# Transposes of late tokens issued when they are ready, one norm per group moved to GpSimd, mask loads moved to SyncE, convolution turns taken one chunk sooner

## Chip, cores, metric

One core of a Trainium2 chip. The metric is the device time of one launch in microseconds (us); the profile's span leaves out some 1.8 us of it. Engines: PE (TensorE), ScalarE (ACT in the profile), VectorE (DVE), GpSimd (POOL) and SyncE (SP, which here only issues DMA). The kernel before took 560.66 us (median of 4 runs, 559.19 to 561.94).

## The reference, cut

Four residual layers on a 2048 x 512 bf16 sequence: long convolution (S4), local attention, and both once more with the same weights.

```python
x = A_u
x = x + _A_ref(_layernorm(x), A_re, A_im, B_re, B_im, C_re, C_im, log_dt, Dskip)   # FFT convolution of length 2L
x = x + _B_ref(_layernorm(x), B_wqkv, B_wo)
x = x + _A_ref(...)        # the same again
x = x + _B_ref(...)

def _B_ref(x, wqkv, wo):   # 32 heads of 16; each token sees 8 tokens at distance 0, 2, .., 14
    qkv = (x @ wqkv) ...
    logits = einsum(q, k[idx]) * 16 ** -0.5; masked where idx < 0
    return (softmax(logits) @ v[idx]) @ wo
```

## The kernel before, the parts that matter

The tokens lie in four groups of four slots (512 tokens each). In an attention layer `KS` and `QS` hold the rows of K and Q as the logits read them, `st` the rows on their way there, and `xnT` holds the normalized, transposed tokens (its name in the profile is XU). Groups 0 and 1 (the even half) are made in a prologue, groups 2 and 3 (the odd half) while the loop runs, by `late`. The loop has 36 steps, nine for each of four row sets `n`; sets `n` = 0 and 1 need only groups 0 and 1, sets 2 and 3 need groups 2 and 3.

```python
class LnStats:
    def gather(self, X, part, j0, j1):              # bn_stats on VectorE, one per slot
    def aggregate(self, j0, j1, half=None):         # bn_aggr on VectorE; with half: power 0.5 (a square root, "the power" below) in two GpSimd instructions
    def scales(self, j0, j1):                       # reciprocal and bias on VectorE, after the power
    def norm(self, dst, src, j, eng=None):          # VectorE, or GpSimd if given

# a projection: rows of K or Q for set n; the copies into KS/QS go by SyncE's queue
def proj(n, k, eng=on_dve):
    par, fp = n // 2, n % 2
    ...
    ps = gps([128, 512])
    for ct in range(4):
        nc.tensor.matmul(ps[:], wqk[...], xnT[:, ct, par, ...], ...)
    eng(st[n, which][...], ps[:])
    if h or n == 0:
        for e in range(2):
            nc.sync.dma_start(T[e::2, e, f2, ...], st[n, which][e::2, ...])

# PE, VectorE and ScalarE run in the order written; the order of GpSimd and SyncE is the scheduler's
with tc.manual_schedule(engines={PE, DVE, Activation}):
    def late(t):                                    # called at the end of step t
        for g in (2, 3):
            u, m0 = t - 2 * g + 4, g * 4            # group 2: steps 0..3, group 3: steps 2..5
            if u in (0, 1):   gather two slots, all parts
            elif u == 2:      ln_b.aggregate(m0, m0 + 4, C["half"])
            elif u == 3:
                ln_b.scales(m0, m0 + 4)
                four norms on GpSimd into xq[g]
                two nc.sync.dma_start_transpose(xt[...], xq[g][...])
                four nc.gpsimd.tensor_copy(xnT[...], xt[...])
    ... prologue: norms, transposes on PE, first rows of set 0 ...
    for t in range(36):
        end = min(total, max(need, done + (4 if t < 4 or t >= N - 8 else 3)))   # projection units of this step
        logits(t)            # PE reads KS, QS; exponential on ScalarE
        square()
        work(end - 1, t)
        values(t - 2)        # PE; reciprocal and product on VectorE
        ...
        turn_o(t // 3 - 1)   # every third step: transpose by SyncE, copy by GpSimd
        late(t)
```

The second convolution is a software pipeline over 16 chunks: `s1(k)` first transform (PE, evacuated into a Z tile), `turns(k)` two chunks' transposes by SyncE, `s2`, `product` (VectorE), `inverse`, `final`. Masks (the fixed rows of KS and QS) and two weights were issued from GpSimd's queue (`eng = nc.gpsimd`).

The softmax here doesn't subtract the row's maximum and nothing guards it: scores larger than these inputs give would overflow.

Of the kernel before, what the change touches and what calls it, by code (L numbers as in the profile page):

```python
# [14 lines left out]
BF = mybir.dt.bfloat16  # L15
# [146 lines left out]
def load_b_weights(nc, const, wq_in, C, wqkv, wo):  # L162
# [6 lines left out]
    wsrc = wqkv.rearrange("(t p) f -> p t f", p=128)  # L169
    eng = nc.gpsimd  # L170
    mask = nc.inline_tensor(_bf(_mask_rows()), name="c_mask").ap()
# [522 lines left out]
def kernel_and_first_conv(nc, tc, C, prm, x2d, const, kt_dram, kscr, ln, ln_b, W, wq_src):  # L694
    with ExitStack() as es:
# [100 lines left out]
        with tc.manual_schedule(engines={mybir.EngineType.PE}):  # L796
# [11 lines left out]
            for u in range(2):  # L808
                cv.block(2 + u, xc, Kt, VT, 10 if u == 0 else 4)
            ln_b.gather(X, 0, 0, 8)  # L810
            nc.scalar.activation(cv.one.tile([128, 1], F32, name="pre", tag="pre")[:], C["half"][:, 0:1], ACT.Sqrt)
# [5 lines left out]
def a_layer(nc, tc, C, X, kt_dram, XU, ln_b, finish):  # L817

    with ExitStack() as es:
# [45 lines left out]
        def turns(k):  # L865
            turn(nc, zpair(k), Z[k // 4], (k % 4) * 4, 8)
# [72 lines left out]
        with tc.manual_schedule(engines={mybir.EngineType.PE, mybir.EngineType.DVE, mybir.EngineType.Activation}):  # L939
            s1(0, on_dve)  # L940
            finish()
            s1(1, on_act)
            s1(2, on_dve)
            s1(3, on_act)
            zpair(0)
            warm(2)
            turn_pe(0)
            s1(4)
            s2(0, True)
            turns(2)  # L950
            turn_pe(1)
            for i in range(16):
                if 0 < i < 7:
                    s2(i)
                if 6 <= i < 15:
                    s2(i + 1)
                product(i)
                if i == 15:
                    inverse(14, True)
                    inverse(15)  # L960
                if 0 < i < 15:
                    inverse(i - 1, i > 10)
                if i == 0:
                    s1(5, on_dve)
                if i + 6 < 16:
                    s1(i + 6)
                    if i % 4 == 1:
                        turns(i + 3)
                        turns(i + 5)
                if i >= 5:  # L970
                    final(i - 5, on_dve if i in (6, 8) else on_act)
                if 10 <= i < 14:
                    ln_b.gather(X, 0, 2 * i - 20, 2 * i - 18)
                if i >= 14:
                    ln_b.gather(X, 1, 4 * i - 56, 4 * i - 52)
            for k in range(11, 16):
                final(k)


def b_layer(nc, tc, C, X, Wt, ln_b, XU, store=None, ln_next=None):  # L980

    with ExitStack() as es:
# [40 lines left out]

        def normed(g, acts):
            xn = []
            for i in range(4):
# [5 lines left out]
                else:  # L1032
                    ln_b.norm(xn[i][:], X[:, slot(j), :], j)
            return xn
# [175 lines left out]
        with tc.manual_schedule(engines={mybir.EngineType.PE, mybir.EngineType.DVE, mybir.EngineType.Activation}):  # L1210
# [8 lines left out]
            def late(t):  # L1219
                for g in (2, 3):  # L1220
                    u, m0 = t - 2 * g + 4, g * 4
                    if u in (0, 1):
                        for p in range(len(ln_b.parts)):
                            ln_b.gather(X, p, m0 + 2 * u, m0 + 2 * u + 2)
                    elif u == 2:
                        ln_b.aggregate(m0, m0 + 4, C["half"])
                    elif u == 3:
                        ln_b.scales(m0, m0 + 4)
                        xq[g] = ld.tile([128, 4, D], BF, name="xq", tag="xq")
                        for i in range(4):  # L1230
                            ln_b.norm(xq[g][:, i], X[:, slot(m0 + i), :], m0 + i, nc.gpsimd)
                        xt = ld.tile([128, 16, 128], BF, name="xt", tag="xt")
                        for h in range(2):
                            nc.sync.dma_start_transpose(xt[:, 8 * h:8 * h + 8],
                                                        xq[g][:, 2 * h:2 * h + 2].rearrange("p i d -> p (i d)"))
                        for ct in range(4):
                            dst = xnT[:, ct, g // 2, UF:UF + 1024].rearrange("c (p j) -> c p j", j=8)
# [10 lines left out]
            warm(6)  # L1248
            ln_b.gather(X, last, 4, 8)
            ln_b.scales(0, 4)  # L1250
            xn = normed(0, (3,))
            ln_b.aggregate(4, 8)
            root(1)
            pt0 = turned(xn)
            ln_b.scales(4, 8)
            fan(0, pt0, 0)
            xn = normed(1, (3,))
            warm(4)
            pt1 = turned(xn)
            pre = sm.tile([128, 1], F32, name="pre", tag="pre")  # L1260
            nc.scalar.activation(pre[:], C["half"][:, 0:1], ACT.Exp)
# [10 lines left out]
            odd = begun(3, psO)  # L1272
            placed(0, half[0], FIRST, 512)
            spread(3, odd, on_dve)
            placed(2, half[1], FIRST, 512)
            jobs = []
            for n in range(4):
# [4 lines left out]
                jobs += [(NB * n + b // 2 + 1 + b / 100, 1, vproj(p, n % 2, b), 0 if n < 2 else 13) for b in range(NB)]  # L1282
            jobs += [(N - 9 + .8 * m, 2, out(m), 24) for m in range(8)]
            jobs.sort(key=lambda j: j[0])
# [23 lines left out]
            for t in range(N):  # L1308
                need = max([c for d, c in due if int(d) <= t] + [0])
                end = min(total, max(need, done + (4 if t < 4 or t >= N - 8 else 3)))  # L1310
                if t:
# [138 lines left out]
```

## Time and profile before

| stage of the kernel before | us of the span |
|---|---|
| tables and first convolution, to the first prologue statistic | 256.5 |
| prologue of attention layer 1 | 11.1 |
| layer 1: steps 0-8, step 9, 10-27, 28-34 (exponential to exponential) | 31.05, 3.43, 40.90, 18.38 |
| end of layer 1, to the first product of the second convolution | 23.4 |
| second convolution: product 0 to product 15, then to layer 2's first exponential | 48.4, 16.5 |
| layer 2: the same four stretches, and the tail | 31.90, 3.60, 40.49, 18.07, 15.6 |

An undisturbed step takes 2.23 us, so the nine steps 0 to 8 hold over 10 us too much. The page's group for all 72 exponentials shows it from ScalarE's side: busy time and mean of one, then the idle time ahead of them (up to 0.54 us in an even step is part of it) and who ended it.

```profile
L1121 ACT ACTIVATE PT<-S 128x1824 bf16<-128x1824 f32 x72 | 121.8, 1691 | 52.4 <-PE S L1118 52.2
```

### The profile page before, as it was taken

How to read it: one execution, taken by the hardware profiler on the slowest of the kernel's cores; microseconds unless marked ns; L12 is line 12 of the kernel's file. 1: busy time of each engine (PE TensorE's matmuls, PEld its weight loads, DVE VectorE, ACT ScalarE, POOL GpSimd, SP SyncE). 2: the span in 40 equal slices, each digit the busy share in tenths (PEclk: the TensorE clock that was granted, in tenths of full speed). 3: DMA queues.
4: the chain of work that ended last, by engine and by line, in shares of the span. 5: the costliest groups of instructions: out<-in, count | busy, mean ns of one | idle time of the engine just before them, and what ended most of it. 6: DMA issues, size and time to landing. Idle time of an engine off the chain costs nothing.

```text
span 559.4 us, 15229 instructions
## 1 busy us (share of the span) xinstructions
PE 394.0 (70%) x6465; PEld 259.0 (46%) x6526; DVE 429.3 (77%) x967; ACT 354.5 (63%) x435; POOL 85.2 (15%) x137
## 2 busy tenths in 40 slices
PE   0200665585668459698976999777897797699977
PEld 0100433464337136465544566545565554366654
DVE  4999999979989998776863666576978787266753
ACT  4999554355536247356654778966877766378771
POOL 0000000000000020533084101250000207411110
PEclk9999997789779688799997999887989999699999
DMA  8201057532463557344134334125863013434542
GB/s 275 110 1 37 2 113 98 85 124 54 99 115 114 115 80 223 53 150 153 67 81 114 87 69 87 15 85 115 170 132 66 2 57 73 110 77 86 115 68 77
DMA packets 99896, 52.51 MB, mean 94 GB/s; under 512 B 85235, under 2 KB 92788, under 8 KB 98548
## 3 DMA queue, kind: packets, MB, share of 16 engines
q1 hardware_dynamic: 97316, 47.73, 37.1%
q0 software_dynamic: 928, 3.41, 1.9%
q8 instruction: 51, 0.84, 0.6%
q10 hardware_dynamic: 1584, 0.39, 0.3%
q14 instruction: 17, 0.14, 0.1%
HBM read 17.96 MB, written 8.13 MB: 47 GB/s over the span
## 4 chain that ended last, share of the span: by engine, by line
PE 36%; DVE 22%; ACT 10%; DMA 5%; issue 3%; POOL 3%; SPq 2%; ACTq 0%; DVEq 0%; POOLq 0%
PE psG L1083 6%; ACT PT L1121 6%; DMA zt<-Z 5%; PE psG L1101 4%; PE S L1118 4%; PE O L1137 4%; PE psG L1172 3%; DVE Ytab L656 3%; DVE Y2tab L658 3%; DVE ln_st_b L212 2%; DVE ta L619 2%; DVE tb L620 2%; POOL XU L1238 1%; SPq L266 1%; POOL xq L260 1%
## 5 line engine op out<-in xcount | busy, mean ns | idle before, releaser
L1121 ACT ACTIVATE PT<-S 128x1824 bf16<-128x1824 f32 x72 | 121.8, 1691 | 52.4 <-PE S L1118 52.2
L1087 DVE CAST st<-psG 128x512 bf16<-128x512 f32 x56 | 38.3, 684 | 37.1 <-PE psG L1083 37.1
L1083 PE MATMUL psG<-XU,wqk 128*128 128x512 bf16 x196 | 57.8, 395 | 3.7 <-issue 1.6
L1118 PE MATMUL S<-QS,KS 32*128 32x114 bf16 x1152 | 28.8, 214 | 24.9 <-DMA KS<-st 15.7
L1137 PEld LDWEIGHTS <-PT 128*128 128x128 bf16 x1152 | 39.4, 97 | 13.9 <-DVE on L1145 2.5
L1118 PEld LDWEIGHTS <-KS 32*128 32x128 bf16 x1152 | 20.4, 94 | 49.5 <-issue 38.0
L1137 PE MATMUL O<-V,PT 128*128 128x17 bf16 x1152 | 40.4, 171 | 0.8 <-DVE on L1145 0.3
L1101 PE MATMUL psG<-wv,XU 128*128 128x256 bf16 x288 | 39.6, 273 | 0.6 <-ACT V L1103 0.6
L307 PE MATMUL psA<-X,sb_F 128*128 128x128 bf16 x128 | 13.5, 238 | 36.4 <-ACT X L720 35.2
L307 PEld LDWEIGHTS <-sb_F 128*128 128x128 bf16 x256 | 17.4, 106 | 43.6 <-issue 41.2
L1141 DVE RECIPROCAL rd<-O 128x16 f32<-128x16 f32 x72 | 18.2, 253 | 21.1 <-PE O L1137 19.3
L294 ACT CAST Z<-psA 128x1024 bf16<-128x1024 f32 (+1 forms) x32 | 28.8, 984 | 7.8 <-PE psA L307 7.8
L1145 DVE TENSOR_TENSOR on<-O,rd 128x256 bf16<-128x256 f32 x72 | 30.5, 424 | 2.5
L678 PE MATMUL psk<-Y2tab,Xtab 128*32 128x48 bf16 x1024 | 22.8, 202 | 12.4 <-issue 10.3
L675 PE MATMUL psk<-Ytab,Xtab 128*32 128x64 bf16 x1024 | 23.6, 206 | 11.1 <-issue 6.0
L332 PE MATMUL psA<-zt,sb_C 128*128 128x512 bf16 x30 | 15.8, 554 | 21.4 <-DMA zt<-Z 21.4
L656 DVE TENSOR_TENSOR Ytab<-Ytab,MA 128x2048 bf16<-128x2048 bf16 (+1 forms) x33 | 30.6, 928 | 0.2
L1154 POOL COPY oT<-oS 128x684 bf16<-128x684 bf16 x20 | 15.2, 759 | 101.6 <-DMA oS<-on 101.6
L658 DVE TENSOR_TENSOR Y2tab<-Ytab,MB 128x2048 bf16<-128x2048 bf16 (+1 forms) x33 | 30.6, 927 | 0.0
L633 POOL MEMSET Xtab<- 128x64 bf16 x8 | 1.6, 202 | 182.3 <-PE psk L678 154.8
L1101 PEld LDWEIGHTS <-XU 128*128 128x128 bf16 x288 | 25.5, 98 | 7.6 <-issue 1.3
L684 ACT CAST KTq<-psk 128x1024 bf16<-128x1024 f32 (+1 forms) x9 | 8.3, 918 | 32.7 <-issue 32.1
(248 smaller groups left out, 1084.9 us busy)
## 6 DMA issues: line engine op xcount, KB each, us to landing
kt_scratch<-Kt SPq DMA_DIRECT2D x4, 1024.0 KB, 3.9
Kt<-kt_scratch SPq DMA_DIRECT2D x4, 1024.0 KB, 5.3
QS<-st SPq DMA_DIRECT2D x24, 128.0 KB, 2.1
KS<-st SPq DMA_DIRECT2D x24, 128.0 KB, 2.1
X<-in_A_u_dram SPq DMA_DIRECT2D x4, 512.0 KB, 5.6
out_dram<-X SPq DMA_DIRECT2D x16, 128.0 KB, 1.8
k_scratch<-KTq SPq DMA_DIRECT2D x7, 256.0 KB, 2.4
KT<-k_scratch SPq DMA_DIRECT2D x7, 256.0 KB, 2.9
```

Of the source, the lines that this page charges most:

```text
L294: self.nc.scalar.copy(dst, src)
L307: nc.tensor.matmul(o, F1[:, j, r, :], rhs_j(j), start=True, stop=not dk)
L656: nc.vector.tensor_tensor(v(Y[:, :, :, q * EYB:(q + 1) * EYB, :]), src, vm(self.mult(self.MA, lev, hc, EYB)), ALU.mult)
L658: nc.vector.tensor_tensor(v(Y2[:, :, :, (q - 1) * EYB:q * EYB, :]), src, vm(self.mult(self.MB, lev, hc, EYB)), ALU.mult)
L675: nc.tensor.matmul(psk[32 * g:32 * g + 32, ds, :], xs, Y[:, m // 2, h, :, t], start=(m == 0), stop=False, skip_group_check=True)
L1083: nc.tensor.matmul(ps[:], wqk[:, ct, f0:f0 + 128], xnT[:, ct, par, UF + h * 512:UF + h * 512 + 512], start=(ct == 0), stop=(ct == 3))
L1087: eng(st[n, which][:, h * 512:h * 512 + 512], ps[:])
L1101: nc.tensor.matmul(ps[:].rearrange("p h d -> p (h d)"), xnT[:, ct, par, NQ * b + 1:NQ * b + 1 + NK], wv[:, ct, fp * 256:fp * 256 + 256], s ...
L1118: nc.tensor.matmul(S[:, i, sl * NQ:(sl + 1) * NQ], KS[r, e, f2, b * NQ + 1:b * NQ + 1 + NK], QS[r, e, f2, UF + b * NQ:UF + b * NQ + NQ], s ...
L1121: nc.scalar.activation(pt[:, 0:16 * NQ].rearrange("k (i x) -> k i x", i=4), S[:, :, 0:4 * NQ], ACT.Exp, scale=DH ** -0.5)
L1137: nc.tensor.matmul(O[:, x * 8 + i * 2 + e, :], pt[:, c0:c0 + 128], V[:, par * NB + b, (fp * 2 + f2) * 8 + i * 2 + e, :], start=True, stop= ...
L1145: nc.vector.tensor_tensor(on.rearrange("q (h d) -> q h d", d=DH), O[:, :, 0:DH], rd[:].unsqueeze(2).to_broadcast([128, 16, DH]), ALU.mult)
```

## The change

Its intent: (1) issue the transposes of groups 2 and 3 as soon as their tokens are normalized, and start group 2 two steps sooner by taking its statistics before the loop; (2) relieve VectorE in the prologue by one norm per group on GpSimd; (3) to free GpSimd for that, issue masks and weights from SyncE; (4) run the convolution's first transform one chunk further ahead, so that its SyncE transposes can be issued sooner; (5) even out the work in the loop's last steps.

```diff
--- before.py
+++ after.py
@@ -167,7 +167,7 @@
     wo_t = const.tile([128, 4, 512], BF, name="wo_t")
     sets.append([const.tile([128, 2, 2, UW], BF, name=f"{nm}1") for nm in ("KS", "QS")])
     wsrc = wqkv.rearrange("(t p) f -> p t f", p=128)
-    eng = nc.gpsimd
+    eng = nc.sync
     mask = nc.inline_tensor(_bf(_mask_rows()), name="c_mask").ap()
     def fringe(u):
         for w, T in enumerate(sets[u]):
@@ -807,7 +807,7 @@
                           lambda c: cv.block(c, xc, Kt, VT))
             for u in range(2):
                 cv.block(2 + u, xc, Kt, VT, 10 if u == 0 else 4)
-            ln_b.gather(X, 0, 0, 8)
+            ln_b.gather(X, 0, 0, 12)
             nc.scalar.activation(cv.one.tile([128, 1], F32, name="pre", tag="pre")[:], C["half"][:, 0:1], ACT.Sqrt)
             nc.sync.dma_start(kt_dram[3], Kt[:])
             cv.final(3, 0, 128, Xr, VT, lambda j0, j1: None, warm=8)
@@ -949,32 +949,34 @@
             s2(0, True)
             turns(2)
             turn_pe(1)
+            ahead = {0: (5, 6), 1: (7, 8)}
             for i in range(16):
                 if 0 < i < 7:
                     s2(i)
                 if 6 <= i < 15:
                     s2(i + 1)
                 product(i)
-                if i == 15:
-                    inverse(14, True)
-                    inverse(15)
-                if 0 < i < 15:
+                if 0 < i:
                     inverse(i - 1, i > 10)
-                if i == 0:
-                    s1(5, on_dve)
-                if i + 6 < 16:
-                    s1(i + 6)
-                    if i % 4 == 1:
-                        turns(i + 3)
-                        turns(i + 5)
+                for k in ahead.get(i, (i + 7,)):
+                    if k < 16:
+                        s1(k, on_dve if k == 5 else on_act)
+                if i in (1, 4, 8):
+                    k = i // 4 * 4 + 4
+                    turns(k)
+                    turns(k + 2)
                 if i >= 5:
                     final(i - 5, on_dve if i in (6, 8) else on_act)
                 if 10 <= i < 14:
                     ln_b.gather(X, 0, 2 * i - 20, 2 * i - 18)
-                if i >= 14:
-                    ln_b.gather(X, 1, 4 * i - 56, 4 * i - 52)
-            for k in range(11, 16):
+            final(11)
+            ln_b.gather(X, 1, 0, 3)
+            inverse(15)
+            ln_b.gather(X, 1, 3, 8)
+            ln_b.gather(X, 0, 8, 12)
+            for k in range(12, 16):
                 final(k)
+            ln_b.gather(X, 1, 8, 12)
 
 
 def b_layer(nc, tc, C, X, Wt, ln_b, XU, store=None, ln_next=None):
@@ -1021,7 +1023,7 @@
         def sps(shape, dt=F32):
             return psS.tile(shape, dt, name="S4", tag="S4")
 
-        def normed(g, acts):
+        def normed(g, acts, pools):
             xn = []
             for i in range(4):
                 xn.append(xnp.tile([128, D], BF, name="xn", tag="xn"))
@@ -1030,7 +1032,7 @@
                     nc.scalar.activation(xn[i][:], X[:, slot(j), :], ACT.Identity, bias=ln_b.nb[:, j:j + 1],
                                          scale=ln_b.rstd[:, j:j + 1])
                 else:
-                    ln_b.norm(xn[i][:], X[:, slot(j), :], j)
+                    ln_b.norm(xn[i][:], X[:, slot(j), :], j, nc.gpsimd if i in pools else None)
             return xn
 
         def turned(xn):
@@ -1217,22 +1219,25 @@
             xq = {}
 
             def late(t):
-                for g in (2, 3):
-                    u, m0 = t - 2 * g + 4, g * 4
-                    if u in (0, 1):
+                for g, steps in ((2, (0, 1, 2, 4)), (3, (4, 5, 7, 8))):
+                    m0 = g * 4
+                    if g == 3 and t in (2, 3):
                         for p in range(len(ln_b.parts)):
-                            ln_b.gather(X, p, m0 + 2 * u, m0 + 2 * u + 2)
-                    elif u == 2:
+                            ln_b.gather(X, p, m0 + 2 * t - 4, m0 + 2 * t - 2)
+                    if t == steps[0]:
                         ln_b.aggregate(m0, m0 + 4, C["half"])
-                    elif u == 3:
+                    elif t == steps[1]:
                         ln_b.scales(m0, m0 + 4)
                         xq[g] = ld.tile([128, 4, D], BF, name="xq", tag="xq")
                         for i in range(4):
                             ln_b.norm(xq[g][:, i], X[:, slot(m0 + i), :], m0 + i, nc.gpsimd)
-                        xt = ld.tile([128, 16, 128], BF, name="xt", tag="xt")
+                    elif t == steps[2]:
+                        xt = xq[g, 1] = ld.tile([128, 16, 128], BF, name="xt", tag="xt")
                         for h in range(2):
                             nc.sync.dma_start_transpose(xt[:, 8 * h:8 * h + 8],
                                                         xq[g][:, 2 * h:2 * h + 2].rearrange("p i d -> p (i d)"))
+                    elif t == steps[3]:
+                        xt = xq[g, 1]
                         for ct in range(4):
                             dst = xnT[:, ct, g // 2, UF:UF + 1024].rearrange("c (p j) -> c p j", j=8)
                             nc.gpsimd.tensor_copy(dst[:, :, (g % 2) * 4:(g % 2) * 4 + 4],
@@ -1246,17 +1251,20 @@
             ln_b.aggregate(0, 4)
             root(0)
             warm(6)
-            ln_b.gather(X, last, 4, 8)
+            ln_b.gather(X, last, 4, 6)
             ln_b.scales(0, 4)
-            xn = normed(0, (3,))
+            xn = normed(0, (2,), (3,))
+            ln_b.gather(X, last, 6, 8)
             ln_b.aggregate(4, 8)
             root(1)
             pt0 = turned(xn)
+            ln_b.gather(X, last, 8, 10)
             ln_b.scales(4, 8)
             fan(0, pt0, 0)
-            xn = normed(1, (3,))
+            xn = normed(1, (2,), (3,))
             warm(4)
             pt1 = turned(xn)
+            ln_b.gather(X, last, 10, 12)
             pre = sm.tile([128, 1], F32, name="pre", tag="pre")
             nc.scalar.activation(pre[:], C["half"][:, 0:1], ACT.Exp)
             fan(1, pt1, 0)
@@ -1271,8 +1279,8 @@
             logits(0)
             odd = begun(3, psO)
             placed(0, half[0], FIRST, 512)
+            placed(2, half[1], FIRST, 512)
             spread(3, odd, on_dve)
-            placed(2, half[1], FIRST, 512)
             jobs = []
             for n in range(4):
                 p = n // 2
@@ -1280,7 +1288,7 @@
                     k0 = i + 4 if n == 0 else i
                     jobs.append((NB * n - 2.5 + (k0 // 4 * 4 if n else 4 + i // 2), 2, proj(n, k), 0 if n < 2 else 13))
                 jobs += [(NB * n + b // 2 + 1 + b / 100, 1, vproj(p, n % 2, b), 0 if n < 2 else 13) for b in range(NB)]
-            jobs += [(N - 9 + .8 * m, 2, out(m), 24) for m in range(8)]
+            jobs += [(N - 8 + .75 * m, 2, out(m), 24) for m in range(8)]
             jobs.sort(key=lambda j: j[0])
             due = [(d, sum(j[1] for j in jobs if j[0] <= d)) for d, *_ in jobs]
             total = due[-1][1]
@@ -1307,7 +1315,7 @@
                 omm(tail[m], m, (0, 1))
             for t in range(N):
                 need = max([c for d, c in due if int(d) <= t] + [0])
-                end = min(total, max(need, done + (4 if t < 4 or t >= N - 8 else 3)))
+                end = min(total, max(need, done + (4 if t < 4 else 3)))
                 if t:
                     logits(t)
                 square()
```

## The prediction

> **What bounds the kernel now.** I read the page's groups first, then the waits by stage, then the timelines of the queues named there. The kernel has four stages: tables and first convolution (0 to 257 us), first attention layer (257 to 373), second convolution (373 to 438), second attention layer (438 to 559.4). In an attention layer PE, ScalarE and VectorE share a loop of 36 steps (step t: logits, exponential, values, a slice of projection work), and no engine is full there. In the groups one line has a long wait on a transfer:
>
> ```profile
> L1118 PE MATMUL S<-QS,KS 32*128 32x114 bf16 x1152 | 28.8, 214 | 24.9 <-DMA KS<-st 15.7
> ```
>
> The logits idle 15.7 us for key rows to land. The waits of each attention layer put nearly all of it on one event per layer, the logits of step 9, the first to use the second set of rows:
>
> ```profile
> PE S L1118 <- DMA KS<-st: 7.1, 1, 7.1
> ```
>
> ```profile
> 480.50 0.28 PE L1118 MATMUL S<-QS,KS 32*128 32x114 bf16 x4 [7.94 <-DMA KS<-st]
> ```
>
> (The first line is layer 1's wait, the second the PE timeline of layer 2.) SyncE's queue in layer 1 shows why the rows are late: one of two KS copies stands behind two transposes (L1234) of normalized tokens.
>
> ```profile
> 281.69 2.74 SPq L1234 DMA_TRANSPOSE xt<-xq  x2
> 287.15 0.55 SPq L1092 DMA_DIRECT2D KS<-st  x1
> 292.89 2.73 SPq L1234 DMA_TRANSPOSE xt<-xq  x2
> 295.68 0.58 SPq L1092 DMA_DIRECT2D KS<-st  x1
> ```
>
> GpSimd's timeline shows what the second transposes waited for:
>
> ```profile
> 277.52 1.04 POOL L226 TENSOR_TENSOR ln_den_b<-ln_mv_b,half 128x4 bf16<-128x4 f32 x1
> 280.15 3.02 POOL L260 TENSOR_SCALAR xq<-X,ln_rstd_b,ln_nb_b 128x512 bf16<-128x512 bf16 x4 [1.58 <-DVE ln_nb_b L231]
> 286.55 4.11 POOL L1238 COPY XU<-xt 128x512 bf16<-128x512 bf16 x4 [1.99 <-DMA xt<-xq]
> 290.61 0.75 POOL L1154 COPY oT<-oS 128x684 bf16<-128x684 bf16 x1
> 291.36 3.00 POOL L260 TENSOR_SCALAR xq<-X,ln_rstd_b,ln_nb_b 128x512 bf16<-128x512 bf16 x4
> ```
>
> One serial chain: statistics of group 2 aggregated at 276.72 (VectorE), power, four norms, transposes, four copies, norms of group 3 done at 294.4, transposes, then KS at 295.68 and logits at 298.06: 21.3 us. Everything from step 9 on hangs on its start. The same chain stands in layer 2 (459.08 to 481.0).
>
> In the second convolution PE waits twice for transposes which SyncE issues only when the last chunk of a Z tile is evacuated:
>
> ```profile
> 405.95 0.39 PE L881 MATMUL psB<-zt,sb_C 128*128 128x512 bf16 x1 [1.55 <-DMA zt<-Z]
> 422.12 0.39 PE L881 MATMUL psB<-zt,sb_C 128*128 128x512 bf16 x1 [2.78 <-DMA zt<-Z]
> 424.89 0.69 DVE L894 TENSOR_TENSOR pa<-xc,Kt 128x1024 bf16<-128x1024 bf16 x1 [1.56 <-ACT xc L886]
> 401.15 6.17 SPq L266 DMA_TRANSPOSE zt<-Z  x4
> 417.48 6.12 SPq L266 DMA_TRANSPOSE zt<-Z  x4
> ```
>
> **The Trainium skill.** "DMA: Bandwidth & Descriptors", section "Anatomy of one DMA — SWDGE (gpsimd) path", says that DMA engines do not wait on semaphores; the wait sits on the issuing sequencer before dispatch. The trace agrees: KS stood 8 us in SyncE's queue, then landed about 2.1 us after its issue. The same section gives about 2.0 us fixed plus bytes over 436 GB/s; here 1 MB copies take 3.9 to 5.3 us. "TensorE: Matmul & The Clock Gate", section "What's actually happening", halves the clock after an idle window of about 3.4 us; after the convolution's first stall, which is only 2 us, consecutive 256-column matmuls start 0.21 us apart instead of 0.11, so the trace agrees on the factor and shows that a shorter gap can coincide with it. "GPSIMD Engine Reference", section "4.1 Engine selection", calls one-input elementwise work roughly line-rate on GpSimd; here one 128x512 norm takes 0.76 us there against about 0.43 on VectorE and 0.81 on ScalarE.
>
> **The change part by part.**
>
> 1. *Tokens of group 2 earlier.* Their statistics leave steps 0 and 1 and are taken before: eight instructions, 2.8 us of VectorE by the timeline (1.40 + 1.39), in layer 1. Four of them (about 1.9 us) go into a VectorE gap of 2.48 us at 244.7 in the first convolution, hidden; four of 128 columns (0.8 us) into the layer's prologue. In layer 2 they go to the convolution's end and the prologue. Group 2 is aggregated at step 0 instead of 2: after the first cast of step 0, about 270.8 instead of 276.72, 5.9 us sooner. Rebuilding the chain from durations above: aggregate 0.4, power 1.3 (to 272.5), reciprocal and bias with a VectorE cast ahead (273.2), norms 3.0 (276.3), second transpose landing 3.2 after its issue (279.6), copies 4.1 (283.7). The instruction order shows one loss: group 3's power now stands behind these copies, 1.3 us (285.0); then oT 0.75, norms 3.05 (288.9), transpose issue 1.25 (290.1), KS twice at 0.55, landing 2.1 after the second's issue: 292.8. Both KS copies still stand behind group 3's transposes in SyncE's order, so a stall of some 3.5 us stays. The chain is 22.0 us against 21.3: gain 5.9 - 0.7 = 5.2 us, in each attention layer, so 10.4.
>
> 2. *Prologue.* One of VectorE's three norms per group goes to GpSimd and one from index 3 to 2 on ScalarE; half the second group's statistics go behind the norms. VectorE's path to the last fan-out loses 2 x 0.43 and gains 0.8 of statistics, and the first norms start 0.4 sooner: about 0.5 us, already inside 5.9. The swapped row placement lets a PSUM bank go 0.6 sooner at step 0 (PE idles 0.46 there), also inside it.
>
> 3. *Convolution.* s1 runs one chunk further ahead and turns for chunks 8 and 12 come one step sooner. Transposes for 8 could be issued at about 399 instead of 401.15 and land before PE asks at 404.2; those for 12 at about 412 to 414 instead of 417.48, landing before 419.3. PE's waits of 1.55 + 0.46 and 2.78 + 0.45 go, with the slow clock behind the first. What reaches the end is less, since VectorE was busy during the first: products of steps 8 and 9 start 5.6 us apart where neighbours take 3.2 (2.4 lost), and VectorE idles 1.56 before step 12. Sum 4.0. One more Z evacuation (1.0 us on ScalarE) at step 1 costs perhaps 0.6 but comes back at step 9. At the end two of six X casts move into ScalarE's idle 1.76, but VectorE gets 2.2 us of statistics, which I count as even. Gain 4.0.
>
> 4. *Loop end.* By the job list, steps 28 and 29 do 3 units instead of 4, the last two go to step 33, which had none. Steps 28 to 30 took 2.6 us each against 2.23 for an even one: two times 0.37, about 0.7 per layer, 1.4. The last square comes one step later; GpSimd's norms for the convolution then end near 372.3 on the old scale, before PE's 372.96: hidden.
>
> 5. *Masks by SyncE.* GpSimd sheds 8 mask issues of about 0.62 and two weight issues of 0.77, 6.5 us, none on the path but needed so that its new norms are free. The price: on SyncE wo_t stands first and waits for the first convolution's last matmul (about 257.8; its memory is reused), so set 0's masks leave at 258.4 to 260.8 instead of 235.7 to 239.3. wo_t plus set 0 are 1.65 MB; at an estimated 350 GB/s (436 in the skill's formula, derated) they land near 264.2, and the first predicated copy wants them near 264.9. I charge 0.4 us for the chance that they are late.
>
> Sum: 10.4 + 4.0 + 1.4 - 0.4 = 15.4 us; 560.87 - 15.4 = 545.5.
>
> **Rivals.** *The stall returns in full:* the order keeps KS behind group 3's transposes, so if GpSimd's chain slips by a few us (reciprocal at step 5 waiting for the late power, the oT copy waiting for its own transpose), parts 2 and 1 are eaten. For it: GpSimd is serial and every link counts twice, once per layer. Against: aggregation moves two steps for sure. At half the gain: 551. *Masks become the wait:* landing 2 us late moves the whole of layer 1 by 2 us: 547.5; layer 2 is untouched, as masks load once. *VectorE or ScalarE bounds the convolution:* then the removed PE waits are worth 1.5 instead of 4: 548. *The better case:* the stall vanishes since other work lets KS go sooner: another 7 us, 539; the order of SyncE speaks against it.
>
> **Range and chances.** The first and second rivals cost up to 6 us, some unseen slack gives up to 4: 541 to 551. A fall of 2% is 549.7, which needs 11.2 of the 15.4 us: 0.83 for faster, 0.16 for within 2%, 0.01 for slower.
>
> **What would show it.** Right: PE's wait for KS falls from 7.1 and 7.9 to 3 to 4 us each; group 2's aggregate stands about 6 us earlier before step 9; KS still issued right behind L1237's transposes; no PE wait over 1 us for zt in the convolution, whose span falls by about 4; steps 28 to 30 near 2.3. Wrong: first predicated copies waiting for a mask; logits of step 6 waiting for rows of set 0, whose last two pairs now stand behind group 2's transposes (they should land at 281.3, needed near 282); or the step-9 wait unchanged because GpSimd's chain only moved its idle time.

## The result, and the profile after

The changed kernel took 544.03 us (median of 4 runs, 542.3 to 547.12) beside 560.66 us: ratio 0.971, 95% interval 0.966 to 0.976, faster. All ratios here are the mean time of one kernel's fast runs over the mean of the other's in the same rounds, so they are not quite the ratio of the quoted medians. In a later session of five rounds it took 540.98 us beside 558.33 (0.9675, 0.9641 to 0.9709).

Stage by stage, from the profiled runs (the profile of the changed kernel fell on its fastest run, span 540.5):

| stage | before | after | change |
|---|---|---|---|
| front (tables, first convolution) | 256.50 | 255.11 | -1.39, not told from chance |
| prologue 1 | 11.10 | 10.53 | -0.57 |
| layer 1: steps 0-8 | 31.05 | 25.87 | -5.18 |
| step 9 | 3.43 | 2.23 | -1.20 |
| 10-27 | 40.90 | 40.76 | -0.14 |
| 28-34 | 18.38 | 17.70 | -0.68 |
| end of layer 1 | 23.41 | 23.92 | +0.51 |
| convolution, products | 48.42 | 43.83 | -4.59 |
| convolution, end and prologue 2 | 16.53 | 17.47 | +0.94 |
| layer 2: steps 0-8 | 31.90 | 26.60 | -5.30 |
| step 9, 10-27, 28-34, tail | 77.78 | 76.48 | -1.30 |

The change touches the front too (four statistics more, masks by SyncE), but three kernels with the front of the kernel before took 256.50, 255.13 and 253.01 us for it (the kernel before, the loop's end alone, the convolution alone), so its 1.39 us are within the variation.

The groups of the logits and of the exponentials after (the line numbers moved by two), to set beside the prediction's first line and the line above:

```profile
L1123 ACT ACTIVATE PT<-S 128x1824 bf16<-128x1824 f32 x72 | 121.7, 1691 | 39.5 <-PE S L1120 39.2
...
L1120 PE MATMUL S<-QS,KS 32*128 32x114 bf16 x1152 | 28.2, 211 | 13.3 <-DMA KS<-st 6.6
```

The wait for KS fell from 15.7 to 6.6 us, and ScalarE's idle time from 52.4 to 39.5. PE's waits of layer 1 and then of layer 2 (us in total, times, longest):

```profile
PE S L1120 <- DMA KS<-st: 2.5, 2, 2.2
```

```profile
PE S L1120 <- DMA KS<-st: 4.1, 3, 2.8
```

So 7.1 and 7.9 became 2.2 and 2.8, a little less than the 3 to 4 predicted. SyncE's queue shows that the order is as predicted, KS right behind group 3's transposes, and the PE timeline the logits which waited for it:

```profile
272.71 2.73 SPq L1237 DMA_TRANSPOSE xt<-xq  x2
...
285.48 2.73 SPq L1237 DMA_TRANSPOSE xt<-xq  x2
288.30 1.18 SPq L1094 DMA_DIRECT2D KS<-st  x2
```

```profile
290.55 0.23 PE L1120 MATMUL S<-QS,KS 32*128 32x114 bf16 x4 [2.20 <-DMA KS<-st]
```

GpSimd's timeline of layer 1 is the chain of the prediction's part 1, link by link: power of group 2, its norms, the copies, group 3's power (behind the copies, as the prediction's working had it); the norms of group 3 follow at 283.94.

```profile
269.57 1.01 POOL L226 TENSOR_TENSOR ln_den_b<-ln_mv_b,half 128x4 bf16<-128x4 f32 x1
271.17 3.01 POOL L260 TENSOR_SCALAR xq<-X,ln_rstd_b,ln_nb_b 128x512 bf16<-128x512 bf16 x4 [0.58 <-DVE ln_nb_b L231]
277.53 4.12 POOL L1243 COPY XU<-xt 128x512 bf16<-128x512 bf16 x4 [3.35 <-DMA xt<-xq]
...
282.01 1.02 POOL L226 TENSOR_TENSOR ln_den_b<-ln_mv_b,half 128x4 bf16<-128x4 f32 x1
```

From the aggregate (268.79, VectorE) to the logits of step 9 it took 21.8 us (22.0 were predicted), and it began 3.15 us after the layer's first exponential instead of 9.12. One new wait is in it: VectorE stood still for the late power, and everything that it should have evacuated stood behind it.

```profile
283.07 0.18 DVE L230 RECIPROCAL ln_rstd_b<-ln_den_b 128x4 f32<-128x4 bf16 x1 [2.13 <-POOL ln_den_b L226]
```

In the convolution the transposes left SyncE at 390.46 and 402.92, and PE's longest wait for zt is 0.3 us:

```profile
390.46 6.89 SPq L266 DMA_TRANSPOSE zt<-Z  x4
```

```profile
PE psB L882 <- DMA zt<-Z: 0.3, 1, 0.3
```

Products 8 to 9 stand 3.20 us apart instead of 5.60, products 11 to 12 2.65 instead of 4.30; products 1 to 2 3.52 instead of 2.60, the price of the earlier Z evacuation. Two places got slower. At the end of layer 1 VectorE waits for the power of the sums that the last, later square completes, and PE behind it; at the end of the convolution VectorE has seventeen statistics in one piece, and PE waits for the norms after them, 2.30 us where it waited 0.90 us in the kernel before (first VectorE's timeline, then PE's; at 356 to 358 and at 423 to 429):

```profile
356.64 0.20 DVE L255 RECIPROCAL ln_rstd_a<-ln_den_a 128x8 f32<-128x8 bf16 x1 [1.97 <-POOL ln_den_a L251]
...
423.43 3.91 DVE L212 BATCH_NORM_STATS2 ln_st_b<-X 128x6 f32<-128x128 bf16 x17
```

```profile
357.72 0.31 PE L1166 MATMUL psG<-sb_ident,on 114*128 114x114 bf16 x2 [1.67 <-DVE on L1147]
...
429.02 1.67 PE L1042 MATMUL S<-sb_ident,xn 128*128 128x128 bf16 x16 [2.30 <-DVE xn L260]
```

### The profile page after: what moved, and what is told of

Read it like the earlier page. It is cut to its first block, busy times and chain, and to the rows that moved or that the text cites. A ratio compares the mean times of both kernels' runs of the same rounds, so it can differ in the third digit from the quotient of the medians.

```text
span 540.5 us, 15231 instructions
## 1 busy us (share of the span) xinstructions
PE 389.8 (72%) x6464; PEld 257.8 (48%) x6526; DVE 428.1 (79%) x963; ACT 354.8 (66%) x435; POOL 81.5 (15%) x131
## 4 chain that ended last, share of the span: by engine, by line
PE 38%; DVE 24%; ACT 9%; DMA 5%; issue 3%; SPq 1%; POOL 0%; ACTq 0%; DVEq 0%
PE psG L1085 7%; ACT PT L1123 6%; PE psG L1103 5%; PE S L1120 5%; PE O L1139 4%; DMA zt<-Z 3%; DVE Ytab L656 3%; DVE Y2tab L658 3%; PE psG L1174 2%; DVE ln_st_b L212 2%; PE S L1174 2%; DVE ta L619 2%; DVE tb L620 2%; DMA KS<-st 1%; DVE pa L894 1%
## 5 line engine op out<-in xcount | busy, mean ns | idle before, releaser
L1123 ACT ACTIVATE PT<-S 128x1824 bf16<-128x1824 f32 x72 | 121.7, 1691 | 39.5 <-PE S L1120 39.2
L1085 PE MATMUL psG<-XU,wqk 128*128 128x512 bf16 x196 | 56.6, 386 | 2.3 <-issue 1.4
L678 PE MATMUL psk<-Y2tab,Xtab 128*32 128x48 bf16 x1024 | 22.9, 202 | 11.7 <-issue 9.6
```

Of the source, the lines that this page charges most:

```text
L1085: nc.tensor.matmul(ps[:], wqk[:, ct, f0:f0 + 128], xnT[:, ct, par, UF + h * 512:UF + h * 512 + 512], start=(ct == 0), stop=(ct == 3))
L1123: nc.scalar.activation(pt[:, 0:16 * NQ].rearrange("k (i x) -> k i x", i=4), S[:, :, 0:4 * NQ], ACT.Exp, scale=DH ** -0.5)
```

## The experiments

My theory: the gain in the attention layers comes from the earlier start of a serial chain on GpSimd and SyncE, the rest from the convolution, and the parts add up. The rivals: the place of KS in SyncE's queue matters rather than the start; or the parts depend on each other. Eleven kernels ran, all correct and all profiled. The first four do one part each on the kernel before (three rounds; before 560.01 us median of 7).

### One part alone: the tokens

```diff
 # kernel before, plus from the change: the new late(t), gather(X, 0, 0, 12) in the first convolution,
 # group 2's other statistics at the second convolution's end and in the prologue
-                for g in (2, 3):
+                for g, steps in ((2, (0, 1, 2, 4)), (3, (4, 5, 7, 8))):
```

> Only the earlier tokens (statistics of group 2 before the loop, aggregate at step 0, transposes and copies in steps of their own), on the kernel before; masks and norms stay where they were. Theory: this part carries the attention layers, so step 0 to step 9 falls by about 5 us in each (31.05 to 26, 31.90 to 26.7), the rest is unchanged apart from up to 0.9 us more at the convolution's end for the moved statistics; total about -9 to -11 us. Rival (the norms and masks off GpSimd are what makes it possible): step 0 to 9 falls by under 2.5 us per layer.

Measured: 554.27 us, ratio 0.9886 (0.9829 to 0.9944). Layer 2's steps 0 to 8 fell by 4.34 us, but layer 1's by only 2.16, as the rival had it, so the total missed the 9 to 11 us expected. SyncE's queue in layer 1 shows the larger part of why:

```profile
275.23 1.25 SPq L1237 DMA_TRANSPOSE xt<-xq  x1
276.59 1.17 SPq L1094 DMA_DIRECT2D KS<-st  x2
277.85 2.04 SPq L1237 DMA_TRANSPOSE xt<-xq  x1
```

The scheduler put a KS copy between group 2's two transposes. The copies on GpSimd then began 14.9 us after the first exponential; in the full change they begin at 11.9 (0.6 of these 3 us arose before the transposes, at the power). Group 3's power stands behind the copies, VectorE waited for it, and the casts that PE needed waited behind. PE's waits in this layer show none for KS; the longest was for such a cast (VectorE's timeline, PE's waits):

```profile
287.10 0.18 DVE L230 RECIPROCAL ln_rstd_b<-ln_den_b 128x4 f32<-128x4 bf16 x1 [4.66 <-POOL ln_den_b L226]
```

```profile
PE psG L1103 <- DVE st L1089: 3.3, 1, 3.3
```

The same edit is worth 2 or 4 us according to where it falls in a queue that the edit does not name. Beside this, the profiled run lost 2.1 us in the second convolution's products (50.51 us instead of 48.42), where the edit changes nothing: after its second stall the granted clock was 0.50 (420 to 422), where it stood at 1.00 in the kernel before.

### One part alone: the convolution

```diff
 # kernel before, plus the change's loop in a_layer, without the statistics of slots 8 to 11
+            ahead = {0: (5, 6), 1: (7, 8)}
...
+                if i in (1, 4, 8):
+                    turns(...)
```

> Only the convolution's new order, on the kernel before. Theory: product 0 to product 15 falls from 48.4 us to about 43.8, both waits for zt gone, total -4 to -5 us. Rival (VectorE or ScalarE bounds the stage): PE's waits go but the stretch falls by under 2 us.

Measured: 554.21 us, 0.9886 (0.9828 to 0.9944). Its products take 43.85 us, the changed kernel's 43.83, so this part's 4.6 us are its own. The stretch after them took 15.97 us without the additional statistics (before 16.53, changed 17.47): the convolution gives 0.6 there, and the statistics moved to that end come with the 1.5 us between 15.97 and 17.47. Part of it is the clock, whose mean was 1.00 in the first of these stretches and 0.90 in the second.

### One part alone: masks by SyncE

```diff
-    eng = nc.gpsimd
+    eng = nc.sync
```

> Only the mask and weight loads from SyncE, on the kernel before. Theory: nothing on the path, total within 0.5 us, since set 0's masks land just ahead of the first predicated copy. Rival: the copies wait for the masks, the prologue of layer 1 (first 128-column statistic to first exponential, 11.1 us) grows by 1 to 2 us.

Measured: 558.84 us, 0.9948 (0.987 to 1.0025), so not told apart by time. In the profile the prologue of layer 1 fell from 11.10 to 10.55, which is all that the whole change gains there. What got shorter are VectorE's three norms per group. In the kernel before, layer 1 (masks built beside them), then layer 2 (none); then layer 1 of this kernel:

```profile
258.74 1.35 DVE L260 TENSOR_SCALAR xn<-X,ln_rstd_b,ln_nb_b 128x512 bf16<-128x512 bf16 x3
...
441.31 1.06 DVE L260 TENSOR_SCALAR xn<-X,ln_rstd_b,ln_nb_b 128x512 bf16<-128x512 bf16 x3
```

```profile
257.72 1.06 DVE L260 TENSOR_SCALAR xn<-X,ln_rstd_b,ln_nb_b 128x512 bf16<-128x512 bf16 x3
```

In the kernel before GpSimd built mask transfers from 258.75 to 259.98 and mask and weight transfers from 260.86 to 262.86, and the two groups of norms, at 258.74 and 261.68, lie beside just these. The Trainium skill's page "SBUF — State Buffer", section "SBUF: two separate sides", says that VectorE and GpSimd share a pair of ports under an exclusive lock and that, where VectorE's instruction is of a kind that needs both ports, whichever starts first keeps it for its instruction. The trace agrees with the consequence, 0.25 to 0.29 us for three norms; the lock itself, and whether these norms are of that kind, it does not show. In the changed kernel the same pattern stands between norms: in the first group VectorE's two norms take 0.73 us and GpSimd's one 1.08, in the second, where GpSimd starts first, 1.01 and 0.76.

### One part alone: the loop's end

```diff
-            jobs += [(N - 9 + .8 * m, 2, out(m), 24) for m in range(8)]
+            jobs += [(N - 8 + .75 * m, 2, out(m), 24) for m in range(8)]
-                end = min(total, max(need, done + (4 if t < 4 or t >= N - 8 else 3)))
+                end = min(total, max(need, done + (4 if t < 4 else 3)))
```

> Only the loop's end (output jobs later, three units a step), on the kernel before. Theory: steps 28 to 35 fall by 0.7 us in each layer, but the last square comes one step later and VectorE's reciprocal for the next norm waits about 2 us for GpSimd's power, so PE waits 1.7 us for the last value tile at the end of layer 1: total about 0 to -1 us. Rival (the power is hidden, as predicted): no such PE wait, total -1.4.

Measured: 558.65 us, 0.9969 (0.9909 to 1.0028). Steps 28 to 34 fell by 0.55 and 0.74 us, the end of layer 1 grew by 0.18. VectorE waited 1.36 us there for the power, but the PE wait of 1.7 us that I expected behind it did not appear. As a gain of 1.3 us in the loop it is seen in the stages, in the time it is below what these rounds resolve.

The four parts sum to 3.1% by their ratios, the whole is 2.9%. That looks like plain addition; the next seven runs show that it is not, in the attention layers. They had five rounds each. The first four shared 558.33 us (median of 11) for the kernel before, the last three 560.81.

### Control

> Control: the changed kernel again, beside the versions built on it, so that they can be compared on the same chip. Expected: 542 to 546 us median, ratio to the kernel before 0.965 to 0.975; the logits of step 9 wait some 2.2 us (layer 1) and 2.8 us (layer 2) for KS, the PE of layer 1's end 1.7 us for the last values.

Measured: 540.98 us, 0.9675 (0.9641 to 0.9709); the front took 253.60 us, the other stages agree with the first profile within 0.35 us but one: step 9 of layer 1 took 3.40 us instead of 2.23 after a stall of the same 2.19 us. The matmuls behind the stall ran at half speed in this run (granted clock 0.50 from 290.2 to 292.2) and not in the other (1.00). So the 1.2 us of step 9 in the table above come and go with the clock. The PE wait of 1.67 us at the end of layer 1, which I expected here too, did not come back: VectorE waited 1.36 us for the power, while PE was busy without a gap at a clock of 0.50 (353 to 357).

### SyncE in written order, on top of the change

```diff
-        with tc.manual_schedule(engines={PE, DVE, Activation}):
+        with tc.manual_schedule(engines={PE, DVE, Activation, SP}):
```

> The changed kernel with one difference: SyncE issues in the order in which the program is written, so KS of the second set stands ahead of group 3's transposes. My theory: what is left of the step-9 wait (2.2 and 2.8 us of PE) is only the place of KS behind those transposes; it goes, and the two layers together lose 4 to 6 us: 538 to 540.5 us against 544 for the changed kernel. Rival: group 3's tokens, whose transposes now stand behind KS, or group 2's behind the rows of set 0, come late in turn and the wait moves to steps 13 to 15 or to step 6: within 1.5 us of the changed kernel.

Measured: 543.03 us, 0.9715 (0.9677 to 0.9753): no gain, my theory missed as written. PE's wait for KS in layer 1 is gone, but another stands in its place, in VectorE's timeline and in PE's waits:

```profile
284.41 0.18 DVE L230 RECIPROCAL ln_rstd_b<-ln_den_b 128x4 f32<-128x4 bf16 x1 [5.10 <-POOL ln_den_b L226]
```

```profile
PE psG L1103 <- DVE st L1089: 3.8, 1, 3.8
```

VectorE runs in written order, so while the reciprocal of group 3 waits for GpSimd's power, the casts of the next rows wait too, and without the casts there are no KS copies to issue. The power waits in turn behind group 2's copies on GpSimd.

### The order alone, on the kernel before

```diff
-        with tc.manual_schedule(engines={PE, DVE, Activation}):
+        with tc.manual_schedule(engines={PE, DVE, Activation, SP}):
 # in late(t): group 3's norms stay at step 5, its transposes and copies go to step 8
+                        if g == 3:
+                            continue
...
+                    elif g == 3 and t == 8:
```

> The kernel before with the order alone: statistics, power and norms of both groups stay where they are, but group 3's transposes and copies come three steps later and SyncE issues in written order, so that KS need not stand behind them. Theory that the change's gain is the earlier start of the chain: order alone gives the larger part of the step-9 wait too, since KS waits for group 2's rows no longer than the chain of group 2 alone (aggregate to copies 13 us): about -4 us per layer, of which some returns at step 13 when group 3's rows come late; 550 to 555 us, PE's wait at step 9 falls from 7.1 and 7.9 to under 4. Rival, that only the start matters: the wait at step 9 stays above 6 us and the time within 2 us of the kernel before.

Measured: 546.62 us, 0.9774 (0.974 to 0.9808), better than the 550 to 555 expected. Two small edits, none of the earlier statistics, give 12 of the changed kernel's 17 us; what each of the two gives by itself was not run. Steps 0 to 8 fell to 23.30 and 24.52 us, further than in the changed kernel (25.87, 26.60); PE's longest waits for KS are 0.3 and 0.9 us. SyncE now issues KS at 284.39 and group 3's transposes at 290.24:

```profile
284.39 1.69 SPq L1092 DMA_DIRECT2D KS<-st  x2
...
290.24 3.34 SPq L1245 DMA_TRANSPOSE xt<-xq  x2
```

The rows of set 1 were ready long before: KS leaves 19.5 us after the layer's first exponential instead of 28.1; they need no token of groups 2 and 3. Against that, steps 10 to 27 grew from 40.90 to 45.13 (layer 2: from 40.49 to 43.32), since group 3's tokens are now late at step 13, where PE waits for their copies:

```profile
298.72 0.38 PE L1083 MATMUL psG<-XU,wqk 128*128 128x512 bf16 x1 [0.63 <-POOL XU L1249]
```

Behind these short waits, none over 0.63 us, the granted clock was 0.50 from 300 to 304, so a part of the 4.2 us is the slow clock. That is what the earlier start of the change is good for: with the order mended, it is worth up to 4.2 and 2.8 us per layer.

### The reciprocal and the norms behind the last values

```diff
+            if ln_next is not None:
+                nc.scalar.activation(pre[:], C["half"][:, 0:1], ACT.Sqrt)
+            values(N - 1)
             if ln_next is not None:
                 ln_next.scale_sums(0, 8)
                 for m in range(8):
                     unorm(m, nc.gpsimd)
-                nc.scalar.activation(pre[:], C["half"][:, 0:1], ACT.Sqrt)
-            values(N - 1)
```

(ScalarE's square root, which the expectation names too, stays ahead of the values in the edit that ran.)

> The changed kernel with the square root and the eight norms of the first half for the convolution put behind the last values of layer 1. My theory: the late last square makes the reciprocal on VectorE wait 2.0 us for GpSimd's power at the head of the layer's end, and PE waits 1.7 us behind it; with the values first, the stretch from the last exponential to the first product of the convolution falls from 23.9 to 22.6 to 23.4 us, so 0.5 to 1.3 us in all: 542.7 to 543.5 us. Rival: the norms on GpSimd then end later and the convolution waits for them instead: equal or up to 1 us slower.

Measured: 540.68 us, 0.9672 (0.963 to 0.9714), the same as the control. VectorE's wait for the power is gone (1.36 us in the control), but the end of layer 1 takes 24.10 us (control 23.61): PE now waits 2.59 us instead of 2.08 for the first Z tile. My theory missed. The PE wait at 357 that it set out to remove stands in the first profile of the changed kernel only; the control had none, so there was little to win.

### Both orders, on top of the change

```diff
-        with tc.manual_schedule(engines={PE, DVE, Activation}):
+        with tc.manual_schedule(engines={PE, DVE, Activation, SP, Pool}):
-                for g, steps in ((2, (0, 1, 2, 4)), (3, (4, 5, 7, 8))):
+                for g, steps in ((3, (3, 5, 7, 8)), (2, (0, 1, 2, 3))):
```

> The changed kernel with two things together: SyncE in written order (KS of the second set ahead of group 3's transposes, as in the version with the order alone changed) and GpSimd in written order with group 3's power written one step sooner, ahead of group 2's copies. Theory: two obstacles stand one behind the other. With KS first alone, VectorE's reciprocal of group 3 still waits 5.1 us for the power behind group 2's copies and holds up the next row casts; with both gone step 9 should not wait at all: exponentials of steps 7 to 9 at 2.2 to 2.7 us each, the first nine steps take 22 to 23.3 us instead of 25.9 and step 9 itself 2.2 instead of 3.4, no new wait at steps 13 to 15. Sum 8 to 10 us against the changed kernel of the same chip (about 531 to 533 us, ratio to the kernel before 0.948 to 0.955). Rival: group 2's or group 3's tokens come late in their turn (steps 13 to 22 lose what step 9 gains): within 3 us of the changed kernel.

Measured: 532.36 us (527.36 to 534.47), 0.9497 (0.9456 to 0.9538), the best version. Over the same kernel before this is 1.8% below the control (0.9497 / 0.9675 = 0.982, two chips). Steps 0 to 8 take 22.00 and 22.94 us, step 9 2.24 and 2.23, steps 10 to 27 40.76 and 40.16 as in the changed kernel. The KS copies leave ahead of group 3's transposes, and GpSimd does group 3's power ahead of group 2's copies:

```profile
282.70 1.46 SPq L1094 DMA_DIRECT2D KS<-st  x2
...
285.82 2.73 SPq L1238 DMA_TRANSPOSE xt<-xq  x2
```

```profile
277.48 1.02 POOL L226 TENSOR_TENSOR ln_den_b<-ln_mv_b,half 128x4 bf16<-128x4 f32 x1
279.45 4.15 POOL L1244 COPY XU<-xt 128x512 bf16<-128x512 bf16 x4 [0.94 <-DMA xt<-xq]
```

The end of the convolution took 19.25 us here against 17.57 in the control, where the edit moves no instruction. The windows of the two profiles, just ahead of layer 2's first exponential (busy time and count by engine, then granted clock, DMA share, GB/s; first this kernel, then the control):

```profile
428.00:432.00 4.00, 3.78 (x21) 2.44 (x20) 1.89 (x3) 2.02 (x5) 0.00 (x0) 0.50 0.00 0
```

```profile
432.50:436.50 4.00, 4.00 (x29) 2.36 (x27) 3.07 (x7) 2.15 (x5) 0.00 (x0) 0.95 0.00 0
```

The clock stood at half here and had come back there, and 1.7 us of this profile's span are lost with it. Whether the edit has a part in it stays open: the other profile with GpSimd in written order (the next run) has it too, 19.44 us, and the five profiles of the changed kernel's convolution without that order have 17.47 to 17.60.

### GpSimd's order alone

The same without SP in the list of engines: group 3's power ahead of group 2's copies, KS still behind group 3's transposes.

> The same without the SyncE part: only group 3's power ahead of group 2's copies on GpSimd, KS still behind group 3's transposes. Theory: the chain to KS gets shorter by the power's 1.3 us and by the reciprocal's wait, so the step-9 wait shrinks but stays: 1.4 to 2.5 us per layer, 2.8 to 5 in all (about 536 to 538.5 us). If the power is the only obstacle (rival), it does as much as both together.

Measured: 544.73 us, 0.9732 (0.9704 to 0.976): no faster than the control, both expectations missed. VectorE no longer stalls, but the copies now wait for the power, which waits for the aggregate of group 3, and so begin later relative to the layer's first exponential (14.1 us against 11.9). The chain to KS got longer, not shorter: PE's longest waits for KS are 3.7 and 3.8 us.

```profile
286.88 2.73 SPq L1238 DMA_TRANSPOSE xt<-xq  x2
289.71 1.18 SPq L1094 DMA_DIRECT2D KS<-st  x2
```

So either order alone gives nothing (0.9715 and 0.9732 against the control's 0.9675), and both together give 1.8%: two obstacles in series.

### Masks back on GpSimd, in the changed kernel

```diff
-    eng = nc.sync
+    eng = nc.gpsimd
```

> The changed kernel with masks and weights issued by GpSimd again. I predicted that the move to SyncE costs 0.4 us and is needed only to free GpSimd. Theory after the single-part run: the move itself shortens the first prologue by 0.55 us, because VectorE's norms take 1.06 us instead of 1.30 to 1.35 when GpSimd is not building descriptors beside them; and here GpSimd's two norms would queue behind about 6 us of issues. Expected: layer 1's prologue 0.5 to 3 us longer, layer 2's unchanged; total 0.5 to 3 us slower than the changed kernel. Rival (nothing in it): within 0.3 us.

Measured: 547.56 us, 0.9763 (0.973 to 0.9796): 0.9% slower than the control by the ratios of two chips, some 5 us, more than I expected; against the first measurement of the changed kernel (0.971, 0.966 to 0.976) it is not told apart, so the stages have to carry it. Layer 1's prologue is 1.09 us longer and its steps 0 to 8 take 30.09 us instead of 26.01. GpSimd still issued masks and a weight after the layer had begun (first exponential at 265.98):

```profile
269.62 0.77 POOL L190 DMA_DIRECT2D wo_t<-in_B_wo_dram  x1
270.46 0.19 POOL L225 TENSOR_SCALAR ln_mv_b<-ln_mv_b 128x4 f32<-128x4 f32 x1
```

The power of group 2 stands behind them, and SyncE has the same split pair of transposes as in the run with the tokens alone (at 275.65 and 278.27, KS between them); the copies begin 16.1 us after the first exponential, and VectorE waits 4.75 us for group 3's power. So the token part pays in full in layer 1 only with the masks off GpSimd. Of the kernels with early tokens, the two with masks on GpSimd show that split in layer 1 and those with masks on SyncE do not; that the scheduler decides by GpSimd's load is my reading of this, not shown by a run of its own.

## Why the prediction was right, point by point

1. *Tokens, 10.4 us.* Right in size and mechanism: 5.2 and 5.3 us in steps 0 to 8 of the two layers. The start moved by 5.97 us (5.9 predicted), the chain grew to 21.8 us (22.0). The residual stall came out at 2.2 and 2.8 us of PE, not 3.5, as part of the loss went into VectorE's wait of 2.13 us for group 3's power; the version with both orders has neither wait and is 3.9 us shorter in layer 1's steps 0 to 8. That reciprocal was named as a danger in the rivals only. What the prediction had too narrow was the sentence that everything from step 9 on hangs on the chain's start. It hangs on it only because the queue puts KS behind group 3's transposes; the order alone removed the wait (23.30 us), without touching the start. The "better case" that it gave up at 539 us was within reach, by order.
2. *Prologue, 0.5 us.* The size was right (0.57), the cause was not: the masks alone give 0.55, and the moved norms with the added statistics about nothing more (by difference; the norms were not run alone).
3. *Convolution, 4.0 us.* Right: 4.6 us in the products. The early Z evacuation cost 0.9 us at product 1, not 0.6, and the intervals that had held the waits shrank by 2.40, 1.65 and 0.78 us (products 8 to 9, 11 to 12, 14 to 15), more than the 4.0 counted. The statistics at the end, which it counted as even, were not: +0.94 us against the kernel before, about 1.5 against the convolution part alone, a part of it at a slower clock.
4. *Loop end, 1.4 us.* Right: 0.68 and 0.73, with the three steps from 28 on at 2.23, 2.54 and 2.54 us in layer 1 instead of 2.6 each. "Hidden" was wrong for the late last square: the end of layer 1 grew by 0.51, 0.20 and, with this part alone, 0.18 us in three profiles. The stretch varies more than that with the clock: the kernel before took 23.41 us at a mean granted clock of 0.74, the convolution part alone, with the same instructions there, 22.20 at 0.85. So its exact price stays open.
5. *Masks, -0.4 us.* The wrong sign. The first predicated copy found its mask in time (263.44, no wait). On its own the move gained 0.55 us, and within the change it is worth some 5 us in layer 1 (1.09 in the prologue, 4.08 in steps 0 to 8), since without it most of the token part is lost there. The prediction's reading that 1 MB copies take 3.9 to 5.3 us took in the scratch copies only; three 1 MB loads of the same page took 5.8 to 8.4. The prediction said that the move was "needed so that its new norms are free"; what stood behind the masks where they stayed was group 2's power.

The sum was 15.4 us; measured 16.6 by medians. The terms that were off, the prologue's cause, the masks, the convolution's end and the square, are each about a microsecond and partly cancel, which is luck. It is luck too that the mask move, which the prediction booked as a cost, came with the token part. The full stall, late masks and a convolution bound by VectorE did not occur.

## What to carry to other kernels

A wait on a transfer asks two questions: when its data was ready, and what stood ahead of it in the queue of the engine that issued it. Here the data was ready, and moving the entries ahead of it was worth more by itself (11.7 us) than making them sooner by itself (some 6); but an in-order engine that waits (VectorE for a power from GpSimd) can hold the same chain, so look for the second obstacle before judging that the first did not matter. When part of the order is a scheduler's, compare the queues after every edit, also where the edit names nothing in them.

## What the Trainium skill lacked or had wrong

- "SBUF — State Buffer", section "SBUF: two separate sides", has a lock rule for both directions, but its warning tells only of VectorE keeping GpSimd from building a transfer, and the section has no figure for the other. The runs show it: three VectorE norms took 1.35 and 1.30 us while GpSimd built mask and weight transfers, 1.06 and 1.05 without, and the layer's prologue was 0.55 us longer for it.
- "DMA: Bandwidth & Descriptors", section "Anatomy of one DMA — SWDGE (gpsimd) path", says that the wait sits on the issuing sequencer, but in that section not what follows: a ready transfer behind a waiting one waits too. KS copies whose rows were ready waited some 7 us of PE's time per layer here; reordering SyncE's queue, with one group's transposes later, took 12 us off the kernel.
- "TensorE: Matmul & The Clock Gate", section "What's actually happening", gives an idle window of about 3.4 us before the clock halves. Here the same stall of 2.2 us was followed by full speed in one run (step 9: 2.23 us) and by half speed in another (3.40 us), and in the version with the order alone the clock fell to 0.50 behind waits of at most 0.63 us. That short idle times can be enough, and from what length, that section does not say.
- No page read says what scheduling by a compiler does to queues: the same token edit was worth 2.2 us in layer 1 and 4.3 in layer 2, where the order of SyncE differed.
